# A decode attention block with its MLP: twelve of the sixteen key/value units as a hardware loop, the units in another order, and one more transfer for w2

## The chip, the core and the metric

One core of a Trainium2 chip runs the kernel. The metric is device time in microseconds, the median of repeated executions. A profile of one execution belongs to it; its span runs from the first recorded instruction to the last. The engines are called PE (matrix products), DVE (vector work), ACT (activation functions), POOL and SP (the queue that issues nearly all transfers here). Each core has 16 DMA engines, and one transfer is dealt out over all of them.

## The reference

One decode step of a transformer layer for 4 sequences (B = 4, one new token each, D = 640), 32 heads of 128 and a cache of 4096 keys and values per head, all in bf16:

```python
q = (layernorm(x) @ wq).reshape(B, 1, 32, 128)        # no K or V of the new token
scores = einsum("bhqd,bhkd->bhqk", q, k_cache) * 128**-0.5
o = einsum("bhqk,bhkd->bhqd", softmax(scores), v_cache)
h = x + o.reshape(B, 1, 4096) @ wo
a = layernorm(h) @ w1 + b1                             # 640 -> 1728
out = h + (a * tanh(softplus(a))) @ w2                 # mish, 1728 -> 640
```

The two caches hold 134.2 MB each; wq, wo, w1 and w2 hold another 14.9 MB. Everything is read once.

## The kernel before, in words

**Units.** The attention is cut into 16 units (`NU`). A unit is one batch row `b` and a group of 8 heads `o`: 8.39 MB of keys and as many of values. `divmod(u, N)` with N = 4 gives `o, b = u // 4, u % 4`, so the batch row runs fastest. On the chip a unit's block of K or V fills one slot of [128, 32768] bf16: head `h` and sixteenth `p` of its keys make the partition, and the 256 keys of such a sixteenth lie one after the other (64 KB in a row, both in memory and in the slot).

**Slots.** There are three slots (line 70), handed out in turn. The first holds wq to begin with and then V of unit 0; K of units 0 and 1 fill the other two, and K of unit 2 follows K of unit 0. From unit 1 on, V of unit u goes where K of unit u lay, and K of unit u + 2 where V of unit u − 1 lay. The last two slots in turn take the weights for the end (`wend`: wo and w1; `wend2`: w2 and all scratch).

**One unit's work.** `scores(u)` goes through K in four parts of two halves: DVE multiplies a half with the broadcast query (L260, in place), PE adds up the products with eight matmuls against an identity (L267), and DVE reduces each part (L248). `softmax(u)` finds the maximum (L286, two tiny products on PE at L288 and L299, L292 and L301 on DVE) and lets ACT form the exponentials (L306, eight heads). `pv(u)` multiplies them with V in 64 matmuls (L322), and ACT copies the result (L330). `close(u)` sums and divides (L337, L341 on PE, L350 and L351 on DVE) and writes unit u's columns of `otn`. `q_broadcast(u)` makes the broadcast query (a copy on ACT at L221, PE at L226, ACT at L234).

**Order.** The program is written out: all 16 units stand in it one after the other (L360 to L375), and every engine takes its instructions in that order. In unit u: scores(u), with close(u − 2) and q_broadcast(u + 1) between its steps; the load of K for u + 2; softmax(u); pv(u − 1); the load of V for u + 1. Loads wait on SP until their slot is free, and what is behind them on SP waits too. In the profile K of u + 2 is released by pv(u − 1) and V of u by scores(u), and both are issued at L88.

**The end.** wo comes in four transfers (L385), w1 in five (L388), the odd 64 rows of w2 in one (L394), and the thirteen full blocks of w2 in transfers of 6, 6 and 1 blocks (L396, `W2P`). The SP queue has eight landing semaphores that it uses in turn: each transfer here waits until the one eight places before it has landed. Then come the projection with wo (L435), the layer norm, w1 (L488), the activation, w2 (L543), the last sum (L551), a transposing product (L555), a cast (L563) and the output's transfer (L564).

**Instructions.** The engines fetch their own instructions from memory while they run. These fetches go through the same 16 DMA engines; the page lists them as the queues of kind "instruction".

Of the kernel before, what the change touches and what calls it, by code (L numbers as in the profile page):

```python
# [16 lines left out]
def kernel(  # L17
# [24 lines left out]
    NU = NO * N  # L42
    RP = 64
# [17 lines left out]
    W2P = (0, 6, 12, C2)  # L61
# [8 lines left out]
    slots = ctx.enter_context(tc.tile_pool(name="slots", bufs=3))  # L70
    consts = ctx.enter_context(tc.tile_pool(name="consts", bufs=1))
    work = ctx.enter_context(tc.tile_pool(name="work", bufs=2))
    one = ctx.enter_context(tc.tile_pool(name="one", bufs=1))

    x_rows = A_x.rearrange("b s d -> (b s) d")
    out_rows = out.rearrange("b s (c p) -> (b s c) p", p=128)

    def slot(name):
        return slots.tile([128, SLOT], BF16, tag="kv", name=name)

    def load_kv(kind, cache, u, parts=1):
        o, b = divmod(u, N)
        t = slot(f"{kind}{u}")
        tv = t[:, :].rearrange("p (r d) -> p r d", d=Dh)
        view = cache[b, G * o : G * (o + 1)].rearrange("h (p r) d -> (h p) r d", p=PH)
        for i in range(parts):
            r0, r1 = i * R // parts, (i + 1) * R // parts
            nc.sync.dma_start(out=tv[:, r0:r1, :], in_=view[:, r0:r1, :])  # L88
        return tv


    first = slot("first")
# [9 lines left out]
    kts, vts = {}, {}  # L102
    kts[0] = load_kv("kt", A_k_cache, 0)
    kts[1] = load_kv("kt", A_k_cache, 1)
# [14 lines left out]
    otn = consts.tile([128, NO, N, G], BF16)  # L119
    qT = consts.tile([128, H, N], BF16)  # L120
# [28 lines left out]
    ps_cm = tc.tile_pool(name="ps", bufs=1, space=bass.MemoryType.PSUM)  # L149
    ps = ps_cm.__enter__()  # L150

# [5 lines left out]
    for src, dst in ((ln1_v, xT), (x_v, xT_res)):  # L157
        tp_ps = ps.tile([128, DC, N], FP32, tag="oT")
        for c in range(DC):
            nc.tensor.matmul(  # L160
                tp_ps[:, c, :], lhsT=src[:, c, :], rhs=ident[0:N, 0:N], start=True, stop=True
            )
        nc.vector.tensor_copy(out=dst[:, :, :], in_=tp_ps[:, :, :])
# [32 lines left out]
    qT_ps = ps.tile([128, H, N], FP32, tag="qq", name="qT_ps")  # L196
    for h in range(H):
        for c in range(DC):
            nc.tensor.matmul(  # L199
                qT_ps[:, h, :],  # L200
                lhsT=wq_sb[:, c, h * Dh : (h + 1) * Dh],
                rhs=xT[:, c, :],
                start=(c == 0),
                stop=(c == DC - 1),
            )
    nc.scalar.copy(out=qT[:, :, :], in_=qT_ps[:, :, :])
    b_ps = ps.tile([128, FC], FP32, tag="oT", name="b_ps")
# [8 lines left out]
    qbs = {}  # L216

    def q_broadcast(u):
        o, b = divmod(u, N)
        qx = one.tile([128, G, PH], BF16, tag="qx", name=f"qx{u}")  # L220
        nc.scalar.copy(  # L221
            out=qx[:, :, :],
            in_=qT[:, G * o : G * (o + 1), b].unsqueeze(2).to_broadcast([128, G, PH]),
        )
        qb_ps = ps.tile([128, Dh], FP32, tag="qq", name=f"qb_ps{u}")
        nc.tensor.matmul(  # L226
            qb_ps[:, :],
            lhsT=qx[:, :, :],
            rhs=ident[:, :],
            start=True,  # L230
            stop=True,
        )
        qbs[u] = work.tile([128, Dh], BF16, tag="qb", name=f"qb{u}")
        nc.scalar.copy(out=qbs[u][:, :], in_=qb_ps[:, :])  # L234

    vts[0] = load_kv("vt", A_v_cache, 0)
    q_broadcast(0)
    q_broadcast(1)


    s_sbs, e2s, rss, o_sbs = {}, {}, {}, {}

    def scores(u):
        s_sbs[u] = one.tile([128, R], FP32, tag="s_sb", name=f"s_sb{u}")
        before = None

        def reduce(part, s_ps):
            nc.vector.tensor_reduce(  # L248
                out=s_sbs[u][:, part * RP : (part + 1) * RP],
                in_=s_ps[:, :, :],  # L250
                axis=AX.X,
                op=ALU.add,
            )

        for part in range(NP):
            kt = kts[u][:, part * RP : (part + 1) * RP, :]
            s_ps = ps.tile([128, RP, W], FP32, tag="s", bufs=4, name=f"s{u}_{part}")
            for k in range(NQ):
# [4 lines left out]
                    in1=qbs[u][:, d0 : d0 + DQ].unsqueeze(1).to_broadcast([128, RP, DQ]),  # L263
                    op=ALU.mult,
                )
                for d in range(d0, d0 + DQ, W):
                    nc.tensor.matmul(  # L267
                        s_ps[:, :, :],
                        lhsT=ident[:, :],
                        rhs=kt[:, :, d : d + W],  # L270
                        start=(d == 0),
                        stop=(d == Dh - W),
                    )
                if before is not None:
                    reduce(*before)
                    before = None
                yield
            before = (part, s_ps)
        reduce(*before)
        kts.pop(u)  # L280
        qbs.pop(u)

    def softmax(u):
        s_sb = s_sbs.pop(u)
        pm = one.tile([128, 1], FP32, tag="pm", name=f"pm{u}")
        nc.vector.tensor_reduce(out=pm[:, :], in_=s_sb[:, :], axis=AX.X, op=ALU.max)  # L286
        tr_ps = ps.tile([128, 128 + G], FP32, tag="tr", name=f"tr{u}")
        nc.tensor.matmul(  # L288
            tr_ps[0:1, 0:128], lhsT=pm[:, :], rhs=ident_f[:, :], start=True, stop=True
        )  # L290
        mx = one.tile([1, G], FP32, tag="mx", name=f"mx{u}")
        nc.vector.tensor_reduce(  # L292
            out=mx[:, :],
            in_=tr_ps[0:1, 0:128].rearrange("o (a b) -> o a b", a=G),
# [3 lines left out]
        nb_ps = tr_ps[:, 128 : 128 + G]  # L298
        nc.tensor.matmul(nb_ps, lhsT=nscale[:, :], rhs=mx[:, :], start=True, stop=True)  # L299
        nb = work.tile([128, G], FP32, tag="nb", name=f"nb{u}")  # L300
        nc.vector.tensor_tensor(out=nb[:, :], in0=nb_ps, in1=own[:, :], op=ALU.add)  # L301
        e2 = work.tile([128, NGV, G, RQ], BF16, tag="e2", name=f"e2_{u}")
        e2s[u] = e2
        rss[u] = work.tile([128, G], FP32, tag="rs", name=f"rs{u}")
        for i in range(G):
            nc.scalar.activation(  # L306
                out=e2[:, :, i, :],
                in_=s_sb[:, :].rearrange("p (g r) -> p g r", r=RQ),
                func=ACT.Exp,
                bias=nb[:, i : i + 1],  # L310
                scale=SCALE,
                accum_out=rss[u][:, i : i + 1],
            )


    def pv(u):
        o, b = divmod(u, N)
        vt, e2 = vts.pop(u), e2s.pop(u)
        o_ps = ps.tile([128, RQ * Dh], FP32, tag="o", name=f"o{u}")
        for g in range(NGV):  # L320
            t = g % CT * (G * RQ)
            nc.tensor.matmul(  # L322
                o_ps[t : t + G * RQ, :],
# [5 lines left out]
        o_sb = one.tile([128, RQ * Dh], FP32, tag="o_sb", name=f"o_sb{u}")  # L329
        nc.scalar.copy(out=o_sb[:, :], in_=o_ps[:, :])  # L330
        o_sbs[u] = o_sb

    def close(u):
        o, b = divmod(u, N)
        o_sb = o_sbs.pop(u)
        oT_ps = ps.tile([128, 2, G], FP32, tag="oT", name=f"oT{u}")
        nc.tensor.matmul(  # L337
            oT_ps[:, 1, :], lhsT=ones_f[:, :], rhs=rss.pop(u)[:, :], start=True, stop=True
        )
        for r in range(RQ):  # L340
            nc.tensor.matmul(  # L341
                oT_ps[:, 0, :],
# [6 lines left out]
        rl = one.tile([128, G], FP32, tag="rl", name=f"rl{u}")  # L349
        nc.vector.reciprocal(out=rl[:, :], in_=oT_ps[:, 1, :])  # L350
        nc.vector.tensor_tensor(  # L351
            out=otn[:, o, b, :], in0=oT_ps[:, 0, :], in1=rl[:, :], op=ALU.mult
# [3 lines left out]
    def close_now(u):  # L356
        for _ in close(u):
            pass

    for u in range(NU):  # L360
        for step, _ in enumerate(scores(u)):
            if u >= 2 and step == 2:
                closing = close(u - 2)
                next(closing)
            if u >= 2 and step == 5:
                next(closing)
            if step == 4 and 1 <= u < NU - 1:
                q_broadcast(u + 1)
        if u + 2 < NU:
            kts[u + 2] = load_kv("kt", A_k_cache, u + 2)  # L370
        softmax(u)
        if u >= 1:
            pv(u - 1)
        if u + 1 < NU:
            vts[u + 1] = load_kv("vt", A_v_cache, u + 1, VQ if u + 1 == NU - 1 else 1)  # L375


    wend = slot("wend")
# [10 lines left out]
    wend2 = slot("wend2")  # L389
# [22 lines left out]
    yT = ps.tile([128, DC, N], FP32, tag="s", bufs=4, name="yT")  # L412

    def regroup(o, b0, b1, o8):
        lm = scratch(N * G * Dh // J, BF16).rearrange("p (b i q) -> p b i q", b=N, i=G)
        o8_ps = ps.tile([128, N, J], FP32, tag="qq", name=f"o8_{o}_{b0}")
# [3 lines left out]
            in0=otn[:, o, b0:b1, :].unsqueeze(3).to_broadcast([128, nb_, G, Dh // J]),  # L420
# [24 lines left out]

    close_now(NU - 2)
    pv(NU - 1)
    dummy = one.tile([N, 1], FP32, name="dummy")
    nc.scalar.activation(out=dummy[:, :], in_=eps_t[0:N, :], func=ACT.Sqrt)
    close_now(NU - 1)  # L450
# [9 lines left out]
    def column_means(src, name):  # L460
# [4 lines left out]
        m_ps = ps.tile([128, N], FP32, tag="oT", name=f"{name}_ps")  # L465
        nc.tensor.matmul(m_ps[:, :], lhsT=mean_f, rhs=part, start=True, stop=True)
# [15 lines left out]
    h1_ps = ps.tile([128, FC, N], FP32, tag="qq", name="h1_ps")  # L482
# [55 lines left out]
    y2T = ps.tile([128, DC, N], FP32, tag="s", bufs=4, name="y2T")  # L538
# [15 lines left out]
    o_ps = ps.tile([N * DC, 128], FP32, tag="tr", name="o_ps")  # L554
# [10 lines left out]
    ps_cm.__exit__(None, None, None)  # L565
# [30 lines left out]
```

## Time and profile before

| | us |
|---|---|
| median of 3 runs | 669.76 (669.63 to 669.79) |
| the profiled execution | 669.93 |
| its span | 668.1 |
| PE busy in it | 387.5 (58%) |
| DVE busy in it | 353.3 (53%) |
| ACT busy in it | 87.1 (13%) |
| bytes read from memory | 283.35 MB, 424 GB/s over the span |

The page cuts the span into 40 equal slices and gives each a digit for the busy share of an engine in tenths:

```profile
PE   0366768376573828557283855728385573828754
DVE  2078848193573819266381836638183664719321
ACT  0102020202011020201102020110202020020211
```

No compute engine is busy throughout. Its digits swing because a unit's work comes when its block has landed.

### The profile page before, as it was taken

Reading aid. Unit: us, or ns where it says so; the run is one execution under the profiler, and the core shown is the slowest. Engines: PE = TensorE matmul, PEld = TensorE weight load, DVE = VectorE, ACT = ScalarE, POOL = GpSimd, SP = SyncE. Lnnn points to the kernel's source line nnn. Section 1 sums busy time; section 2 is a strip of 40 time slices with the busy share of each in tenths; the row PEclk is TensorE's granted clock in tenths of the full one; section 3 lists DMA queues with packets and bytes.
Section 4 is the critical chain, followed back from the end, with each engine's and each line's share of the span. In section 5 each row is a group of like instructions: output and inputs, shape, how many; then the busy total and the mean of one; then the engine's idle time right before and its main releaser. Section 6 shows DMA issues by size and latency. Waiting matters only on the chain.

```text
span 668.1 us, 6433 instructions
## 1 busy us (share of the span) xinstructions
PE 387.5 (58%) x2793; PEld 181.5 (27%) x2793; DVE 353.3 (53%) x314; ACT 87.1 (13%) x314; POOL 1.4 (0%) x10
## 2 busy tenths in 40 slices
PE   0366768376573828557283855728385573828754
PEld 0222323132231313223031322303132231313344
DVE  2078848193573819266381836638183664719321
ACT  0102020202011020201102020110202020020211
POOL 0000000000000000000000000000000000000000
PEclk9999979888697988869696796969789696988865
DMA  9999999999999999999999999999999999999996
GB/s 377 440 436 436 439 433 436 429 428 433 432 433 436 425 436 433 436 433 436 429 436 433 428 436 432 428 440 428 429 432 433 436 436 436 436 432 401 422 417 209
DMA packets 8341, 283.78 MB, mean 425 GB/s; under 512 B 819, under 2 KB 2551, under 8 KB 3192
## 3 DMA queue, kind: packets, MB, share of 16 engines
q1 hardware_dynamic: 8302, 283.35, 98.7%
q8 instruction: 22, 0.36, 0.2%
q14 instruction: 7, 0.06, 0.0%
q10 hardware_dynamic: 10, 0.01, 0.0%
HBM read 283.35 MB, written 0.01 MB: 424 GB/s over the span
## 4 chain that ended last, share of the span: by engine, by line
DMA 60%; DVE 25%; PE 12%; issue 2%; SPq 0%; DVEq 0%
DMA kt<-in_A_k_cache_dram 54%; DVE kt L260 21%; PE s L267 6%; PE o L322 5%; DMA wend<-in_A_wo_dram 4%; DVE s_sb L248 3%; DMA wend<-in_B_w_dram 2%; DVE pm L286 1%; PE tr L288 0%; PE tr L299 0%; DVE mx L292 0%; SPq L385 0%; DVE otn L351 0%; PE y2T L543 0%; DVE rl L350 0%
## 5 line engine op out<-in xcount | busy, mean ns | idle before, releaser
L267 PE MATMUL s<-kt,ident 128*128 128x512 bf16 x1024 | 270.8, 419 | 220.0 <-DVE kt L260 220.0
L260 DVE TENSOR_TENSOR kt<-kt,qb 128x4096 bf16<-128x4096 bf16 x128 | 288.2, 2284 | 189.2 <-DMA kt<-in_A_k_cache_dram 189.2
L267 PEld LDWEIGHTS <-ident 128*128 128x128 bf16 x1024 | 108.7, 106 | 375.8 <-issue 150.1
L306 ACT ACTIVATE e<-s_sb,nb 128x256 bf16<-128x256 f32 x128 | 63.2, 494 | 218.3 <-DVE nb L301 218.3
L248 DVE TENSOR_REDUCE s_sb<-s 128x64 f32<-128x512 f32 x64 | 44.0, 688 | 55.7 <-PE s L267 33.3
L322 PE MATMUL o<-vt,e 128*32 128x512 bf16 x1024 | 68.5, 428 | 3.8 <-DMA vt<-in_A_v_cache_dram 3.8
L234 ACT CAST qb<-qb_ps 128x128 bf16<-128x128 f32 x16 | 4.2, 265 | 305.1 <-PE qb_ps L226 305.1
L322 PEld LDWEIGHTS <-e 128*32 128x32 bf16 x1024 | 29.1, 107 | 35.6 <-issue 16.4
L306 ACT ACTIVATION_READ_ACCUMULATOR e<-s_sb,nb 128x1 f32 x128 | 23.9, 186 | 0.0
L288 PE MATMUL tr<-ident_f,pm 128*1 128x128 f32 x32 | 6.1, 270 | 21.3 <-DVE pm L286 21.3
L341 PE MATMUL oT<-sel,o_sb 128*128 128x8 f32 x128 | 17.5, 263 | 0.7 <-ACT o_sb L330 0.7
L341 PEld LDWEIGHTS oT<-sel,o_sb 128*128 128x128 f32 x128 | 16.4, 201 | 0.9 <-ACT o_sb L330 0.9
L350 DVE RECIPROCAL rl<-oT 128x8 f32<-128x8 f32 x16 | 3.2, 202 | 16.6 <-PE oT L341 16.6
L330 ACT COPY o_sb<-o 128x512 f32<-128x512 f32 x16 | 9.2, 572 | 15.2 <-PE o L322 15.2
L199 PE MATMUL qT_ps<-xT,first 128*128 128x4 bf16 x160 | 4.4, 166 | 11.0 <-DMA first<-in_A_wq_dram 11.0
L288 PEld LDWEIGHTS tr<-ident_f,pm 128*1 128x1 f32 x32 | 1.8, 80 | 28.7 <-issue 28.7
L299 PE MATMUL tr<-mx,nscale 1*128 1x8 f32 x32 | 6.1, 262 | 5.9 <-DVE mx L292 5.9
L292 DVE TENSOR_REDUCE mx<-tr 1x8 f32<-1x128 f32 x16 | 4.5, 279 | 9.0 <-PE tr L288 9.0
L213 DVE COPY b1T<-b_ps 128x13 f32<-128x13 f32 x1 | 0.2, 173 | 14.3 <-PE b_ps L210 14.3
L299 PEld LDWEIGHTS tr<-mx,nscale 1*128 1x128 f32 x32 | 4.7, 183 | 10.6 <-DVE mx L292 10.6
L199 PEld LDWEIGHTS <-first 128*128 128x128 bf16 x160 | 4.3, 104 | 11.0 <-DMA first<-in_A_wq_dram 11.0
L435 PE MATMUL yT<-wend,wend 128*128 128x4 bf16 x160 | 4.9, 167 | 3.8 <-DMA wend<-in_A_wo_dram 3.1
(77 smaller groups left out, 74.7 us busy)
## 6 DMA issues: line engine op xcount, KB each, us to landing
vt<-in_A_v_cache_dram SPq DMA_DIRECT2D x4, 2048.0 KB, 45.1
first<-in_A_wq_dram SPq DMA_DIRECT2D x1, 5120.0 KB, 15.4
wend<-in_A_wo_dram SPq DMA_DIRECT2D x4, 1280.0 KB, 21.8
wend<-in_B_w_dram SPq DMA_DIRECT2D x5, 432.0 KB, 17.4
wend<-in_B_w_dram SPq DMA_DIRECT2D x2, 960.0 KB, 11.4
kt<-in_A_k_cache_dram SPq DMA_DIRECT2D x16, 47.3
vt<-in_A_v_cache_dram SPq DMA_DIRECT2D x15, 34.8
wend<-in_B_w_dram SPq DMA_DIRECT2D x1, 160.0 KB
```

The costliest lines, as they stand in the source:

```text
L199: nc.tensor.matmul(qT_ps[:, h, :], lhsT=wq_sb[:, c, h * Dh : (h + 1) * Dh], rhs=xT[:, c, :], start=(c == 0), stop=(c == DC - 1),)
L248: nc.vector.tensor_reduce(out=s_sbs[u][:, part * RP : (part + 1) * RP], in_=s_ps[:, :, :], axis=AX.X, op=ALU.add,)
L260: nc.vector.tensor_tensor(out=kt[:, :, d0 : d0 + DQ], in0=kt[:, :, d0 : d0 + DQ], in1=qbs[u][:, d0 : d0 + DQ].unsqueeze(1).to_broadcast([1 ...
L267: nc.tensor.matmul(s_ps[:, :, :], lhsT=ident[:, :], rhs=kt[:, :, d : d + W], start=(d == 0), stop=(d == Dh - W),)
L286: nc.vector.tensor_reduce(out=pm[:, :], in_=s_sb[:, :], axis=AX.X, op=ALU.max)
L288: nc.tensor.matmul(tr_ps[0:1, 0:128], lhsT=pm[:, :], rhs=ident_f[:, :], start=True, stop=True)
L299: nc.tensor.matmul(nb_ps, lhsT=nscale[:, :], rhs=mx[:, :], start=True, stop=True)
L306: nc.scalar.activation(out=e2[:, :, i, :], in_=s_sb[:, :].rearrange("p (g r) -> p g r", r=RQ), func=ACT.Exp, bias=nb[:, i : i + 1], scale= ...
L322: nc.tensor.matmul(o_ps[t : t + G * RQ, :], lhsT=e2[:, g, :, :], rhs=vt[:, g * RQ : (g + 1) * RQ, :], start=(g < CT), stop=(g >= NGV - CT),)
L330: nc.scalar.copy(out=o_sb[:, :], in_=o_ps[:, :])
L341: nc.tensor.matmul(oT_ps[:, 0, :], lhsT=o_sb[:, r * Dh : (r + 1) * Dh], rhs=sel[:, r, :], start=(r == 0), stop=(r == RQ - 1),)
L435: nc.tensor.matmul(yT[:, c, :], lhsT=wo_sb[:, o, j, c * 128 : (c + 1) * 128], rhs=o8[:, j, :], start=(o == 0 and j == 0 and c == 0), stop= ...
```

## The change

- **The order of units.** Unit u is now row u of both caches seen as (b, head group): `u // 4` is the batch row and `u % 4` the head group. A block is addressed as rows 128·u to 128·u + 127 of a two-dimensional view, so that u may be a register. `qT` and `otn` are laid out to match, with the batch row outside.
- **The loop.** Units 0, 1, 14 and 15 are written out. Units 2 to 13 run as a loop of four turns with three units each, since the slots repeat after three units. The loop has `iteration_sync="reg_based"`, and a branch hint for PE.
- **Fixed buffers.** Slots, PSUM banks and small tiles are allocated once, by number. The exponentials `e2` and the bias `nb`, which had two buffers, have one; the broadcast query `qb` and the row sums `rs` have three in place of two.
- **Order within a unit.** pv(u − 1) and the loads of V for u and K for u + 2 now come before softmax(u). The order of the loads on SP, and the slots that they use, are those of before.
- **q_broadcast** does its first copy on DVE and no longer on ACT.
- **w2** comes in transfers of 6, 4, 2 and 1 blocks.

```diff
-    W2P = (0, 6, 12, C2)
+    W2P = (0, 6, 10, 12, C2)
+    HINTS = (mybir.EngineType.PE,)
...
-    slots = ctx.enter_context(tc.tile_pool(name="slots", bufs=3))
+    slots = ctx.enter_context(tc.tile_pool(name="slots", bufs=1))
...
+    slot = [slots.tile([128, SLOT], BF16, name=f"slot{i}") for i in range(NS)]
+    banks = [ps.tile([128, 512], FP32, name=f"bank{i}") for i in range(8)]
...
+    def load_kv(rows, u, i, parts=1):
+        w = SLOT // parts
+        for k in range(parts):
+            nc.sync.dma_start(
+                out=slot[i][:, k * w : (k + 1) * w],
+                in_=rows[bass.ds(u * 128, 128), k * w : (k + 1) * w],
+            )
...
+    def q_broadcast(u, i):
+        nc.vector.tensor_scalar(
             out=qx[:, :, :],
-            in_=qT[:, G * o : G * (o + 1), b].unsqueeze(2).to_broadcast([128, G, PH]),
-        )
+            in0=qT[:, bass.ds(u * G, G)].unsqueeze(2).to_broadcast([128, G, PH]),
+            scalar1=1.0,
+            scalar2=None,
+            op0=ALU.mult,
+        )
...
-    for u in range(NU):
-        for step, _ in enumerate(scores(u)):
-            if u >= 2 and step == 2:
-                closing = close(u - 2)
+    def slot_of(u):
+        return 1 if u == 0 else 2 * u % NS
+
+
+    def unit(u, m, first=False, closes=True, last=0):
+        for step, _ in enumerate(scores(1 if first else slot_of(m), m % NS)):
+            if closes and step == 2:
+                closing = close(u - 2, (m - 2) % NS)
                 next(closing)
-            if u >= 2 and step == 5:
+            if closes and step == 5:
                 next(closing)
-            if step == 4 and 1 <= u < NU - 1:
-                q_broadcast(u + 1)
-        if u + 2 < NU:
-            kts[u + 2] = load_kv("kt", A_k_cache, u + 2)
-        softmax(u)
-        if u >= 1:
-            pv(u - 1)
-        if u + 1 < NU:
-            vts[u + 1] = load_kv("vt", A_v_cache, u + 1, VQ if u + 1 == NU - 1 else 1)
+            if step == 4 and last < 2 and m:
+                q_broadcast(u + 1, (m + 1) % NS)
+        if not first and not last:
+            load_kv(v_rows, u, slot_of(m))
+        if last == 1:
+            load_kv(v_rows, u, slot_of(m))
+        if not first:
+            pv(0 if m == 1 else slot_of(m - 1))
+        if last == 1:
+            load_kv(v_rows, u + 1, slot_of(m - 1), VQ)
+        elif not last:
+            load_kv(k_rows, u + 2, slot_of(m + 2))
+        softmax(m % NS)
+
+    LOOP = (2, NU - 2)
+    unit(0, 0, first=True, closes=False)
+    unit(1, 1, closes=False)
+    with tc.For_i(*LOOP, NS, iteration_sync="reg_based", hint_engines=HINTS) as u0:
+        for k in range(NS):
+            unit(u0 + k, LOOP[0] + k)
+    unit(NU - 2, NU - 2, last=1)
+    unit(NU - 1, NU - 1, last=2)
```

## The prediction

> **What bounds the kernel now.** I read the slices and queues first, then DVE's waits, then SP's issues, then the end of the chain.
>
> ```profile
> span 668.1 us, 6433 instructions
> PE 387.5 (58%) x2793; PEld 181.5 (27%) x2793; DVE 353.3 (53%) x314; ACT 87.1 (13%) x314; POOL 1.4 (0%) x10
> DMA  9999999999999999999999999999999999999996
> ...
> q1 hardware_dynamic: 8302, 283.35, 98.7%
> q8 instruction: 22, 0.36, 0.2%
> q14 instruction: 7, 0.06, 0.0%
> ```
>
> The columns of a queue are packets, MB and busy share. The transfers keep all 16 DMA engines busy for 98.7% of the span, from the first microsecond to the last slice. So the bound is the time that DMA engines need for their bytes, and the chain through DVE and PE (54% of it one wait for K) only follows. Two views say by how much compute may come late. The first is the list of waits, the second SP's issues in order of time (start, duration):
>
> ```profile
> DVE kt L260 <- DMA kt<-in_A_k_cache_dram: 189.2, 15, 14.6
> ```
>
> ```profile
> 163.84 0.33 SPq L88 DMA_DIRECT2D kt<-in_A_k_cache_dram  x1
> 195.94 0.33 SPq L88 DMA_DIRECT2D vt<-in_A_v_cache_dram  x1
> 201.99 0.33 SPq L88 DMA_DIRECT2D kt<-in_A_k_cache_dram  x1
> ```
>
> DVE waits 189.2/15 = 12.6 us per unit for K. The K issued at 163.84 lands at 210.67 (46.79 us later in the chain). When V is issued at 195.94, that K still needs 210.67 − 195.94 = 14.7 us, so the engines have 14.7 us of work queued; a later issue costs nothing up to there.
>
> **Which DMA engine is last.** A transfer has landed when the slowest of its 16 shares has. The page gives a mean; the trace's packet records (queue, start, duration, size) give more. A packet of 65536 bytes takes 2421 ns, and on its engine the next starts 3 ns before it ends. So the records can be followed as 16 chains, of which each carries 248 such packets (31 transfers of 128 rows, 8 rows to an engine). They don't finish together:
>
> - six engines that served no instruction fetch: 614.4 to 615.9 us, mean 615.0
> - six that served two fetches of 16384 bytes (q8): 617.7 to 618.2, mean 617.9
> - two that served three of them: 619.4 and 619.5
> - two that served three of 8192 bytes (q14): 616.7 and 617.5
>
> One 16384-byte fetch delays its engine by (617.9 − 615.0)/2 = 1.45 or (619.5 − 615.0)/3 = 1.5 us, and an 8192-byte one by 0.6 to 0.8. The q8 fetches are PE's: 22 for 2 × 2793 recorded instructions, one per 254, and they rotate over eight engines (22.1, 294.6 and 572.0 us are the same engine). The 4.5 us that the slowest engine is behind are still there at the end: the shares of V's last part land over 5.1 us, those of w2's over 5.3.
>
> **The change, part by part.**
>
> *Instruction fetches.* By the counts of the rows a unit costs PE 143 matmuls (64 at L267, 64 at L322, 8 at L341, 2 each at L288, L299 and L337, 1 at L226) and as many weight loads: 286 instructions. Twelve units unrolled are 3432, or 13.5 fetches of 254. One turn of the loop is 858, or 3.4. No run here shows a jump back on PE, so whether the second turn fetches its code again must be bounded. If it doesn't, 22 − 13.5 + 3.4 = 11.9, at most 13, fetches are left: no engine in the rotation of eight serves more than two up to the end of K and V, and the slowest comes 1.5 us earlier. If each of the four turns fetches everything, with one boundary piece and one fetched ahead for nothing, there are 8.5 + 4 × 5.4 = 30: four or five on an engine, 1.5 to 3.0 us later than now. I take −1.5. The row that I lean on is the rotation: eight places of 16384 bytes before one comes round again, and the body takes 3.4 of them, five at most. DVE and ACT have 314 recorded instructions each, some 20 per unit and 60 per turn; their pieces of 8192 bytes come every 130 instructions on DVE, so a turn fits into one or two. Without fetches again they lose one or two of three (−0.6 to −1.6 on two engines that aren't last); two again each turn are 8 × 0.8 = 6.4 us on one engine, 621.4 against 619.5, +1.9.
>
> [...] The trace has the rotation over eight, but no jump.
>
> *Registers, waits and the turn itself.* Each turn adds a jump on five queues, each wait may add register work, and each of the 24 transfers in the loop gets an address from a register. The trace shows none of it. The nearest rows are SP's semaphore instructions (17 to 28 ns) and its issues (328 ns). At nothing it costs 0; at 60 such instructions per unit and 328 ns each, 19.7 us, of which V's 14.7 us would hide most and 5.0 × 12 = 60 us would show. These are plain queue instructions, nearest to the 28 ns row: 60 × 28 = 1.7 us per unit. I take 0; cover is the 14.7 us on SP and the 12.6 on DVE. A jump that waits for code needs a fetch (1.0 to 1.1 us long) behind a 2.4 us packet, about 4 us three times, under the same cover.
>
> *pv(u − 1) ahead of softmax(u), single buffers.* pv takes 3.6 to 5.3 us on PE. The load of K behind it goes out about 2.4 us sooner (in unit 14 scores end at 584.9 and pv begins at 587.3); the exponentials come up to 5.3 us later, and the next to need them is pv(u), a unit later. They may overwrite the one e2 only after pv(u − 1), which PE now does first. Cost 0, cover 12.6 us; without it 16 × 3.6 = 58 us. In unit 15 softmax ends near 635 rather than 630.3; pv(15) then needs 2.8 us for what has landed, and waits for V's last part at 639.6 anyway.
>
> *q_broadcast's copy on DVE, the order of units, fixed banks.* One DVE instruction of 0.2 to 0.3 us per unit (128 × 128 elements; ACT's cast of this size took 0.27) under 12.6 us. Packets stay at 65536 bytes in a row, whichever batch row comes first, and 3968 of them took 2421 ns wherever they lay: 0. The bounds for both are 0 and, uncovered, 16 × 0.3 = 5 us.
>
> *w2 in 6, 4, 2, 1.* The end now:
>
> ```profile
> 661.25 1.16 PE L543 MATMUL y2T<-wend 64*128 64x4 bf16 x35 [2.11 <-DVE wend L534]
> ...
> 663.76 1.09 PE L543 MATMUL y2T<-wend 128*128 128x4 bf16 x35 [1.35 <-DMA wend<-in_B_w_dram]
> 664.89 0.22 DVE L551 TENSOR_TENSOR wend<-wend,y2T 128x20 bf16<-128x20 f32 x1 [3.69 <-PE y2T L543]
> ```
>
> Blocks 6 to 11 land at 663.7 and release 30 matmuls; block 12 lands at 664.1 and has 5 more. With blocks 6 to 9 in a transfer of their own, 20 matmuls (0.6 us) go before 663.7. The rest ends right after the last landing: 664.13 + 5 × 0.031 = 664.3 rather than 664.85, −0.5. The bounds are −0.6 and +0.4 (one more issue, 0.33 to 0.5 us, if SP's queue were late; its last issue now ends at 656.4, 7.7 us before its landing).
>
> **Sum.** −1.5 − 0.5 = −2.0 against a span of 668.1, so 666.1; the profiled execution is 669.93 with 1.8 us around its span, and 0.17 above the median. From the median: 669.76 − 2.0 = 667.7 us. The end is a row of waits for landings (wo 652.3, w1 658.3, w2 663.7), so it moves as a block with the slowest engine.
>
> **Rivals.** A change under 0.2%, 1.3 us, is no change for this kernel.
>
> 1. *Fewer fetches* (forecast): 667.7, own range 665.8 to 668.7. The low end has one fetch less on the slowest engine again. For it: the table by engines, where only fetches separate 615.0 from 619.5. Chance 0.48; 0.44 of it lies beyond 0.2%.
> 2. *As many fetches as now*: the loop fetches 3.4 pieces each turn, 13.5 in all. Only w2's −0.5 is left: 669.3. For it: all 22 fetches in the trace come once per 254 instructions executed, never skipped. Against: straight code can't show anything else. Chance 0.16.
> 3. *More fetches, slower*: at each jump back pieces are thrown away and fetched again, on PE up to 30 in all, on DVE or ACT up to two a turn. The place is the slowest DMA engine, the price 1.5 us a fetch, and it decides from the fourth 16384-byte fetch (or the seventh of 8192) on one engine before V ends. With 4.5 on it: +2.25 − 0.5, 671.5; 670.5 to 673. For it: a jump leaves the sequence in which every fetch here came. Against: the rotation over eight. [...] Chance 0.27, of which 0.02 stays within 0.2%.
> 4. *The turn waits for its transfers*: every engine meets the others and all landings at the jump. Then the queue runs dry: the next V goes out only after 25 us of scores (210.7 to 234.1 and the softmax), so four turns cost 4 × 25 = 100 us, 770 us; a meeting of the engines alone stays under the 14.7 us. The DMA row of the slices would show four gaps. Against: three units share a slot cycle and nothing in it needs the queue empty. Chance 0.07 with other late issues.
>
> The remaining 0.02 are for a faster end that I can't name. Faster: 0.44 + 0.02 = 0.46. Same: 0.04 + 0.16 + 0.02 = 0.22. Slower: 0.25 + 0.07 = 0.32. The range from 665.8 to 672.8 takes in the first three cases but for the top of the third.
>
> **What would show it.** Right: q8 with 11 to 14 packets; the slowest chain of 65536-byte packets ending near 618.0; DMA digits of 9 throughout; PE with two matmul groups at L543 and its equivalent of which the last is short. As many or more than 22 q8 packets point to the second or third case, and q14 above 7 to DVE's or ACT's code. Digits under 9 in the middle of the DMA row, or a K wait on DVE that falls below some 5 us per unit, would show the turn's own cost coming out from its cover. I am wrong altogether if the slowest chain ends where it does now although fetches fell: then the lag of 4.5 us is not theirs.

## The result, and the profile after

The changed kernel takes 694.16 us (median of 6 runs, 693.4 to 694.54) against 669.77 before: a ratio of 1.0362, 95% interval 1.0351 to 1.0373. It is 24.4 us slower. The profiled execution took 693.91 us with a span of 692.1.

The page of the changed kernel, in the lines that answer to those of before:

```profile
span 692.1 us, 7076 instructions
...
PE 374.4 (54%) x2793; PEld 178.6 (26%) x2793; DVE 355.5 (51%) x330; ACT 84.8 (12%) x298; POOL 1.4 (0%) x10
...
DVE  2078847381927557381828466372918300388412
...
DMA  9999999999999999999999999999999999319997
GB/s 406 433 432 421 432 426 439 440 432 429 424 443 424 443 432 436 428 436 432 439 436 428 436 424 443 424 439 436 432 432 424 443 424 443 165 53 414 395 419 254
...
q1 hardware_dynamic: 8318, 283.35, 95.3%
q8 instruction: 12, 0.20, 0.1%
q14 instruction: 5, 0.04, 0.0%
```

Thirty-four slices look as before, and then there is one hole: slices 35 and 36 (588 to 623 us) have DMA digits 3 and 1 and 165 and 53 GB/s in place of some 433. DVE's row has its two zeros just ahead of it. The instruction queues have less to do: 12 packets on q8 in place of 22, 5 on q14 in place of 7.

SP's issues around the hole, in order of time, and the waits of SP and DVE (total us, times, longest):

```profile
543.00 0.33 SPq L92 DMA_DIRECT2D slot<-in_A_v_cache_dram  x1
547.10 0.33 SPq L92 DMA_DIRECT2D slot<-in_A_k_cache_dram  x1
621.27 3.91 SPq L92 DMA_DIRECT2D slot<-in_A_v_cache_dram  x5
```

```profile
SPq L371 <- DMA slot<-in_A_k_cache_dram: 30.4, 2, 19.3
SPq L371 <- DMA slot<-in_A_v_cache_dram: 19.3, 1, 19.3
```

```profile
DVE slot L262 <- DMA slot<-in_A_k_cache_dram: 129.4, 13, 14.1
DVE slot L262 <- PEq L591: 50.2, 1, 50.2
```

L371 is the loop; the trace puts the meeting of the engines behind it at L591. At 547 us SP has issued its last load there (K of unit 15). It then waits for one landing after the other, at 558.9, 578.2 and 597.6 us, and meets the other engines; DVE stands 50.2 us at that meeting ("PEq L591"), although K of unit 14 landed at 558.9. At 598 us all go on, and the DMA engines have nothing left: all three slots are full (K of 14 and 15, V of 13), and in this order none comes free before scores(14) end at 621. By the packet records no data packet runs from 597.1 to 622.2, 25.1 us (the expectations below say 24.9). Before the change V of unit 14 was issued while K of unit 15 was still on its way (the landing of that K and DVE's first use of it, from the chain, and SP's issue):

```profile
552.80 47.79 DMA kt<-in_A_k_cache_dram
600.67 2.30 DVE kt L260
```

```profile
584.90 7.80 SPq L88 DMA_DIRECT2D vt<-in_A_v_cache_dram  x5
```

The landings by the trace's records split the difference of the spans, 692.1 − 668.1 = 24.0 us:

| | before | after | difference |
|---|---|---|---|
| K of unit 15 landed | 600.6 | 597.6 | −3.0 |
| from there to V of unit 14 landed | 19.4 | 47.0 | +27.6 |
| from there to the end | 48.2 | 47.6 | −0.6 |

So the loop was faster while it ran, and lost nine times as much at its end.

### The profile page after: what moved, and what is told of

The parts are those of the page before. It is cut to its first block, busy times and chain, and to the rows that moved or that the text cites. A ratio compares the mean times of both kernels' runs of the same rounds, so it can differ in the third digit from the quotient of the medians.

```text
span 692.1 us, 7076 instructions
## 1 busy us (share of the span) xinstructions
PE 374.4 (54%) x2793; PEld 178.6 (26%) x2793; DVE 355.5 (51%) x330; ACT 84.8 (12%) x298; POOL 1.4 (0%) x10
## 5 line engine op out<-in xcount | busy, mean ns | idle before, releaser
L269 PE MATMUL bank<-slot,ident 128*128 128x512 bf16 x1024 | 268.1, 415 | 272.8 <-DVE slot L262 272.8
L262 DVE TENSOR_TENSOR slot<-slot,qb 128x4096 bf16<-128x4096 bf16 x128 | 288.3, 2285 | 179.6 <-DMA slot<-in_A_k_cache_dram 129.4
L251 DVE TENSOR_REDUCE s_sb<-bank 128x64 f32<-128x512 f32 x64 | 44.0, 688 | 54.3 <-PE L312 23.7
L312 PE MATMUL bank<-slot,e 128*32 128x512 bf16 x1024 | 60.6, 390 | 4.9 <-ACT e L298 3.2
L319 ACT COPY o_sb<-bank 128x512 f32<-128x512 f32 x16 | 9.4, 585 | 197.7 <-PE bank L285 144.9
L325 PE MATMUL bank<-sel,o_sb 128*128 128x8 f32 x128 | 17.4, 263 | 0.4 <-ACT o_sb L319 0.4
L325 PEld LDWEIGHTS bank<-sel,o_sb 128*128 128x128 f32 x128 | 16.4, 201 | 0.5 <-ACT o_sb L319 0.5
L295 PE MATMUL bank<-mx,nscale 1*128 1x8 f32 x32 | 6.1, 262 | 10.3 <-DVE mx L288 10.3
L284 DVE TENSOR_REDUCE pm<-s_sb 128x1 f32<-128x256 f32 x16 | 6.7, 420 | 0.5
L285 PE MATMUL bank<-ident_f,pm 128*1 128x128 f32 x32 | 6.1, 272 | 1.3 <-DVE pm L284 1.3
```

Of the source, the lines that this page charges most:

```text
L251: nc.vector.tensor_reduce(out=s_sb[:, part * RP : (part + 1) * RP], in_=s_bank[part][:, :].rearrange("p (r w) -> p r w", w=W), axis=AX.X, ...
L262: nc.vector.tensor_tensor(out=kt[:, :, d0 : d0 + DQ], in0=kt[:, :, d0 : d0 + DQ], in1=qbs[i][:, d0 : d0 + DQ].unsqueeze(1).to_broadcast([1 ...
L269: nc.tensor.matmul(s_bank[part][:, :].rearrange("p (r w) -> p r w", w=W), lhsT=ident[:, :], rhs=kt[:, :, d : d + W], start=(d == 0), stop= ...
L285: nc.tensor.matmul(tr_bank[0:1, 0:128], lhsT=pm[:, :], rhs=ident_f[:, :], start=True, stop=True)
L312: nc.tensor.matmul(o_bank[t : t + G * RQ, :], lhsT=e2[:, g, :, :], rhs=vt[:, g * RQ : (g + 1) * RQ, :], start=(g < CT), stop=(g >= NGV - CT),)
L319: nc.scalar.copy(out=o_sb[:, :], in_=o_bank[:, :])
```

## The experiments

**The loop written out.** The body of the change stays, only the loop goes:

```diff
-    with tc.For_i(*LOOP, NS, iteration_sync="reg_based", hint_engines=HINTS) as u0:
-        for k in range(NS):
-            unit(u0 + k, LOOP[0] + k)
+    for u in range(*LOOP):
+        unit(u, u)
```

> The changed kernel with its loop written out as twelve units; all else of the change stays. Theory 'exit': the 24.9 us without transfers (597.5 to 622.4) belong to the end of the loop, where SP waits for the last landing. They are gone: DMA digits of 9 to the end, 20 to 23 packets on q8, K of unit 15 landed near 600.6 us as before the change rather than 597.6, span 667 to 668, time 669.3. Rival 'order': the gap comes from pv ahead of softmax, the single buffers or the copy on DVE. Then it stays: span near 692.

Measured: 669.26 us, ratio to before 0.9993 (0.9984 to 1.0002), span 667.5.

```profile
DMA  9999999999999999999999999999999999999996
...
q8 instruction: 22, 0.36, 0.2%
```

The hole is gone and the fetches are back; K of unit 15 is ready for DVE at 600.8 (600.7 before the change). All that the change did besides the loop (the order of pv and softmax, single buffers, the copy on DVE, the units' order) costs nothing that shows. The rival falls.

**Three turns.** The loop ends after unit 10:

```diff
-    LOOP = (2, NU - 2)
+    LOOP = (2, NU - 5)
...
+    for u in range(LOOP[1], NU - 2):
+        unit(u, u)
     unit(NU - 2, NU - 2, last=1)
```

> The changed kernel with three turns (units 2 to 10) and five units written out behind them. Theory 'exit': the gap of some 25 us moves with the end of the loop, three units of 38.7 us earlier, to about 481 to 506 us, and there is none near 597; q8 has 15 to 17 packets; span 692 to 694. Rival 'order' or anything that belongs to units 14 and 15 (four parts of V, the last slots): the gap stays at 597 to 622 us.

Measured: 694.92 us in one run, span 693.1, 15 packets on q8.

```profile
DMA  9999999999999999999999999996079999999997
```

The hole has moved to slices 28 to 30; by the packets it reaches from 481.0 to 507.0, but for two fetches of code. It belongs to the end of the loop, not to the last units.

**The body begun at another point.** Each queue keeps its order; what changes is what lies ahead of the loop's end:

```diff
...
+    def turn_unit(u, m, closes=True):
+        load_kv(v_rows, u, slot_of(m))
+        load_kv(k_rows, u + 2, slot_of(m + 2))
+        softmax(m % NS)
+        score_unit(u + 1, m + 1, closes)
+        pv(slot_of(m))
...
-            unit(u0 + k, LOOP[0] + k)
+            turn_unit(u0 + k, LOOP[0] + k)
...
```

> The loop's body begins at another point: a turn holds, for three units u, the loads of V for u and K for u + 2, softmax(u), scores(u + 1) and pv(u). The order on every queue is that of the changed kernel; only the end of the loop now falls behind scores(14) and pv(13) rather than ahead of them. Theory 'exit': the wait for the last landing is still there (near 597.6), but two slots are free by then, so V of unit 14 goes out some 1 us later and the gap is 2 to 3 us: span 668 to 670, time 669.5 to 671.5. If the gap were the price of the wait itself, whatever stands behind it, it would stay 25 us: span near 692.

Measured: 670.89 us, ratio to before 1.0016 (1.0007 to 1.0025), span 669.1.

```profile
DMA  9999999999999999999999999999999999979997
...
q8 instruction: 12, 0.20, 0.1%
```

```profile
547.55 0.33 SPq L92 DMA_DIRECT2D slot<-in_A_k_cache_dram  x1
598.34 3.32 SPq L92 DMA_DIRECT2D slot<-in_A_v_cache_dram  x5
```

SP still waits for the last landing (597.7), but now V of units 14 and 15 has its slots, and the issue comes at 598.3 rather than 621.3. 2.1 us are without a packet (597.2 to 599.3). So the price isn't that of the wait alone; it is what must be done before the queue can be filled again. The end of the loop still costs more than it saves: K of unit 15 lands 2.9 us earlier than before the change, the last data packet ahead of the output's ends 1.5 us later (665.1 against 663.6), 4.4 us in all. That is 2.1 us of hole. Part of the rest is a slow start: by the packet records the 16 first packets behind the hole begin up to 1.5 us apart (599.3 to 600.8) and last 2.8 to 3.3 us rather than 2.4. How the remainder splits stays open.

**No hint.** `hint_engines=HINTS` is left out of the loop.

> The changed kernel without the branch hint for PE. Theory 'resident': PE's body of some 900 instructions stays where it is, so q8 stays at 12 packets and none falls between 165 and 595 us; span 691.5 to 692.5. Rival 'hint': it is the hint that saves the fetches; without it each jump back fetches 4 or 5 pieces again, q8 has 24 or more, and the slowest DMA engine gets 1 to 3 us more before the loop ends (K of unit 15 at 599 to 601 us rather than 597.6).

Measured: 694.26 us in one run, span 692.5.

```profile
q8 instruction: 12, 0.20, 0.1%
```

By the packet records none of the 12 falls between 159.9 and 599.4 us, while three jumps back are taken. In the changed kernel none falls between 160.0 and 599.3. With the hint or without, the later turns fetched none of PE's code again.

**w2 alone.** In the kernel before:

```diff
-    W2P = (0, 6, 12, C2)
+    W2P = (0, 6, 10, 12, C2)
```

> The kernel before with w2's blocks in transfers of 6, 4, 2 and 1 and nothing else. By the sum: 20 of the last 35 matmuls go ahead of the last landing, -0.5 us, 669.3. If one more issue or landing costs as much as it saves: 669.8.

Measured: 669.47 against 669.92 us in the same set, ratio 0.9993 (0.9984 to 1.0002); the span is 667.6 against 668.1. That is the half microsecond of the sum, though its interval takes in no change.

**More fetches.** In the kernel before, ahead of the product of `q_broadcast`; the result is overwritten by it:

```diff
+        for _ in range(128):
+            nc.tensor.matmul(
+                qb_ps[:, 0:4], lhsT=ident[:, :], rhs=ident[:, 0:4], start=True, stop=True
+            )
         nc.tensor.matmul(
             qb_ps[:, :],
```

> The kernel before with 128 needless matmuls of four columns (and their weight loads) ahead of each broadcast of q: 256 more instructions for PE in each unit, some 4 us under DVE's wait of 12.6. Theory 'a fetch costs its DMA engine 1.5 us': 16 more packets on q8, 38 in all, two more on each of the eight engines, so the slowest ends its 65536-byte packets some 3.0 us later: K of unit 15 lands near 603.6 rather than 600.6, time 672.5 to 673. Rival 'the spread has another cause': the landing stays near 600.6 and the time within 0.5 us of before.

Measured: 672.97 against 669.92 us, ratio 1.0044 (1.0029 to 1.0060): +3.05 us.

```profile
q8 instruction: 38, 0.62, 0.4%
```

Sixteen fetches more, two on each of eight engines, cost 1.5 us each. K of unit 15 is ready at 603.9, 3.2 us later, and the slowest chain of 248 packets of 65536 bytes ends at 622.8 rather than 619.5. So the spread over the engines is that of the fetches, and 0.26 MB among 283 are worth 0.44%.

**Turns parted by a meeting.**

```diff
-    with tc.For_i(*LOOP, NS, iteration_sync="reg_based", hint_engines=HINTS) as u0:
+    with tc.For_i(*LOOP, NS, iteration_sync="barrier", hint_engines=HINTS) as u0:
```

> The changed kernel with the loop's turns parted by a meeting of all engines that clears the semaphores, rather than by waits against registers. Theory 'a meeting waits for every landing, as the one at the end of the loop does': four gaps of some 25 us in the DMA row, each 27.6 us by the landings, so the span is 692.1 + 3 x 27.6 = 775 us. Rival 'only the end waits for landings': one gap as now and the turns' meetings under the cover, 692 to 695 us.

Measured: 777.51 us in one run, span 775.5. The DMA row, and SP's waits in the loop:

```profile
DMA  9999999999997089999914999996099999906997
```

```profile
SPq L371 <- DMA slot<-in_A_k_cache_dram: 119.9, 8, 19.3
SPq L371 <- DMA slot<-in_A_v_cache_dram: 77.2, 4, 19.3
```

Four holes of 25.8 to 26.6 us, and (775.5 − 692.1)/3 = 27.8 us for a turn. SP waits 12 times for landings at L371 (4 turns of three) where the changed kernel does 3 times. So the end of a loop with waits against registers does what each turn of the other kind does: it waits for every landing, and it costs the same, 27.6 and 27.8 us.

**pv first behind the loop.** The first transfer out is V of unit 15, into the slot that pv(13) frees:

```diff
-    unit(NU - 2, NU - 2, last=1)
+    close_now(NU - 4, (NU - 4) % NS)
+    pv(slot_of(NU - 3))
+    load_kv(v_rows, NU - 1, slot_of(NU - 3), VQ)
+    for step, _ in enumerate(scores(slot_of(NU - 2), (NU - 2) % NS)):
+        if step == 4:
+            q_broadcast(NU - 1, (NU - 1) % NS)
+    load_kv(v_rows, NU - 2, slot_of(NU - 2))
+    softmax((NU - 2) % NS)
```

> The changed kernel with another order behind the loop: close(12), pv(13) and the load of V for unit 15 into the slot that this frees come first, and scores(14) with the load of V for unit 14 after them. Theory 'the gap lasts until a slot is free': pv(13) needs its V only, which landed at 578 us, so the first transfer goes out some 4 us after the meeting at 598 and a second, smaller gap of 2 to 3 us opens until scores(14) end near 624: 8 to 9 us idle rather than 24.9, span 675 to 677. If the gap were the price of the meeting: 692.

Measured: 690.05 us in one run, span 688.2. This is a miss. The holes did shrink as expected, to 6.6 and 0.8 us (597.3 to 604.0 and 626.3 to 627.1), but only 3.9 us of the 17.7 came back.

```profile
DMA  9999999999999999999999999999999999598990
```

Two of DVE's rows behind the meeting, in order of time (start, duration; the view ends at 632 us, within the second):

```profile
601.06 6.70 DVE L262 TENSOR_TENSOR slot<-slot,qb 128x4096 bf16<-128x4096 bf16 x3
...
628.58 4.50 DVE L262 TENSOR_TENSOR slot<-slot,qb 128x4096 bf16<-128x4096 bf16 x2
```

The last slice of the DMA row is a 0 now: the last data packet ahead of the output's ends at 673.4, 14.8 us before the span does (4.5 before the change), so the queue no longer sets the end: in the chain all from 660.2 us on is compute. What sets it is the work that stood still: scores(14) could have started at 558.9, when its K had landed, and begins at 601.1; scores(15) follows at 628.6, and its last multiplication at 647.0 comes 27.6 us later than before the change (619.4). The end of the loop empties the queue and holds the compute back at once; mending the first shows the second. In the kernel with the body begun elsewhere both are mended, as scores(14) lie ahead of the meeting: DVE stands 14.3 us there, not 50.2.

## Why the prediction was wrong

It said 667.7 us, between 665.8 and 672.8, and 0.46 for faster; 694.16 was measured, far above the range. Point by point:

- *The bound.* Right: the DMA engines set the end as long as SP issued in time (98.7% busy before the change, 98.8% with the loop written out), and the slowest of 16 is last: before the change its packets of 65536 bytes ended at 619.5 us, those of the first at 614.4.
- *Fetches.* Right in kind, small in size. 12 packets on q8 (11.9 worked out), none inside the later turns. The term was −1.5 us; it measured −3.0 at the landing of K of unit 15. I had counted two fetches for the slowest engine up to the end of V against three; until the loop ends it serves one. The landing of V of unit 13 shows it: the shares of its 16 engines land over 1.9 us (576.3 to 578.2), over 5.1 before (576.1 to 581.2). The third case, in which each jump back fetches PE's code again, falls: three jumps, no packet on q8 between 160.0 and 599.3 us, nor between 159.9 and 599.4 without the hint. That the rotation over eight speaks for this was my estimate: the runs show that this body wasn't fetched again, not why.
- *Registers, waits and the turn itself.* This is the step that failed. The register work did cost nothing that shows: inside the loop the landings keep to 116.2 us per turn of six loads, 19.4 each (before the change DVE's first use of K came 600.67 − 366.84 = 233.8 us later in unit 15 than in unit 9, 116.9 for three units), and DVE still waits 129.4/13 = 10.0 us per unit for K (159.2/15 = 10.6 with the loop written out). But I priced a turn four times, "the turn itself", and the end of the loop not at all. The end costs 27.6 us, and the cover of 14.7 us that I named for SP is of no use where SP waits for the queue to run dry.
- *The fourth rival* had the mechanism and nearly the price (25 us, queue dry, scores first), but at each of four turns, and I set it aside since nothing in a turn needs the queue empty. True for the turns; at the end SP waited for the landings until 597.6, and POOL's clearing of a range of semaphores follows at 597.9 in the trace. Why the landings are waited for there no run shows. With that place it would have read 667.7 + 25 = 692.7.
- *pv ahead of softmax, single buffers, the copy on DVE, the order of units.* Right, nothing: the kernel without the loop is 0.5 us faster than before, within its interval.
- *w2.* The value was −0.5, and alone it measured −0.45.

Two kernels here are nominally faster than before, the one without the loop and the one with w2 alone, each by some 0.5 us, and both intervals take in no change. The loop itself saves 3 us while it runs, and no version of its end that ran here gives less than that back.

## What to carry to other kernels

Price a loop at three places: its entry, its turn and its end. Where the end waits for all landings, the cost begins with the time from the last landing to the first new byte (25.1 us without a data packet in the changed kernel, 2.1 with the body begun at another point), so look at which buffers are free there and which compute is held back; begin the body so that both are done ahead of it, or write the loop out. And in a kernel bound by DMA, look at the 16 engines one by one: here instruction fetches rode on some of them, at 1.5 us for each of 16384 bytes, and the slowest one set the time.

## What the runs showed of the hardware that I hadn't expected

- A fetch of 16384 bytes cost the engine that served it 1.5 us next to packets of 65536 bytes, though its packet lasted 1.0 to 1.1: sixteen more cost 3.05 us, two for each of eight engines.
- A PE body of 858 recorded matmuls and weight loads ran four times without its code being fetched again in the later turns: no packet on q8 between 160.0 and 599.3 us, and without the branch hint none between 159.9 and 599.4.
- The hint, the registers and the jumps of three turns left no trace in the time of a kernel that has 10 to 12 us of cover per unit: 694.26 us in one run without the hint, 694.16 with it; 116.2 us per turn of the loop, 116.9 for three units before the change.
